# A new front with gates on 128 partitions, and VectorE in GpSimd's place for most subtractions

## The chip, the cores and the metric

One NeuronCore of a Trainium2 chip runs the whole program. The metric is the device time of one execution in microseconds, the median of several runs. TensorE (PE in the rows; PEld is its weight load) multiplies, VectorE (DVE) and ScalarE (ACT) do the elementwise work, GpSimd (POOL) helps out, and SyncE (SP) issues the DMAs.

## The reference

An mLSTM attention (batch 2, 8 heads, 768 positions, head size 40) feeds two MLP layers on 1536 tokens of width 320 with an inner width of 2048:

```python
for t in range(S):                                   # attention
    m_new = np.maximum(f_gate[:, :, t] + m, i_gate[:, :, t])
    f_stab = np.exp(f_gate[:, :, t] + m - m_new)
    i_stab = np.exp(i_gate[:, :, t] - m_new)
    C = f_stab * C + i_stab * outer(v_t, k_t);  n = f_stab * n + i_stab * k_t
    y[:, :, t] = sigmoid(o_t) * (C @ q_t) / max(|n @ q_t|, 1)
h = x @ w_in;  x = (h * clip(h + 3, 0, 6) / 6) @ w_out      # layer 1
h = x @ w_in;  out = (h * tanh(softplus(h))) @ w_out        # layer 2
```

(Broadcast indices are left out of the attention lines.)

## The kernel before, in words

**Attention** goes in six chunks of 128 positions (c = 0 to 5), each with two halves of 64. For a chunk, `loads` fetches q and k (`qke`, 1 MB) and then k, v and the o gate with tokens on partitions (`kvo`, 0.97 MB). The gates lie as 16 rows (batch and head) by 768 positions in `gio`. `scan_gates` (L657) runs a scan over them that gives the running maximum `mt`, in three parts (chunk 0, chunk 1, chunks 2 to 5), and follows it with three elementwise operations on the 16 rows; in the second part these three stand on GpSimd. `gates` (L672) transposes the result on TensorE (L679, L680) to 128 partitions by 32, makes the two factors with two sigmoids, a reciprocal and a product (`ist`), transposes the decay back (L701), and scans it over each half (L712 to L716: one scan over 128 columns, with the first column of each half moved to the tile `first`). `decays` spreads the decay into the 64 x 64 triangle of each row by 32 small matmuls and a scan (L840, L842; from chunk 2 on by a DMA through DRAM), `scores` is L815, `carry` builds the state (L942 and the `c` rows), `cross` is L890, `within` L985, and `mixture` (L989) ends with transposes (L1041) that give the layer input `x1` in a pair of fp32r tensors, high part and low part.

**Layers.** Every fp32 product is made of fp32r products of high and low parts. `prep` (L376) fetches a slot of weights (8 slots per layer; `ri` for w_in, 768 KB, `ro` for w_out, 640 KB) into one of four raw buffers, repairs it on ScalarE and VectorE (L365, L367), rounds the high part on ScalarE (L405, L417) and subtracts to get the low part (L411 to L428), on VectorE, GpSimd or TensorE by the lists `pool_rest` and `pe_rest`. The first 512 tokens (chunks 0 and 1) go through layer 1 a chunk at a time (`step1`: `ph` L465 up, `acc` L482 down, 8 slots for each chunk). The other two blocks go 512 wide (`step1_wide`: `phw`, `accw`). `act1` (L541) makes the activation, `r` and its parts `gh` and `gl`; the subtraction for `gl` (L554) stands on VectorE or GpSimd by the list `pool_low`. Layer 2 (`step2`: `qh`, `bcc`) follows for three blocks of 512 tokens.

**The order of the work** on each engine is written by the planner `Flow` while the program is built: every piece of work is a generator that asks for an engine with an estimated time and a priority (the lists in `P`; a lower number goes first), and the planner hands out engines and buffers in the order of its own clock. Engines then run that order strictly. DMAs all leave on the SP queue in planned order. While TensorE has nothing to do before the first `x1`, `keep_warm` (L1189) fills it with products of zeros (`pz`, L1198), as many as the planner's estimate of one fits into the gap.

Of the kernel before, what the change touches and what calls it, by code (L numbers as in the profile page):

```python
# [23 lines left out]
L = 128  # L24
# [17 lines left out]
P = {  # L42
    "const": [22, 11, 148],
    "gates": [81, 93, 41, 162, 127, 206],
    "load": [96, 281, 100, 227, 58, 130],
    "score": [9, 84, 243, 262, 211, 292],
    "value": [1, 29, 209, 138, 45, 241],
    "carry": [106, 73, 77, 59, 249, 250],
    "unit": [19, 171, 75, 86, 244, 228],
# [8 lines left out]
    ],  # L58
    "down2": [
        143, 60, 82, 259, 114, 54, 57, 63, 229, 156, 74, 6, 18, 44, 179, 139, 226, 173, 116, 155, 87, 183,  # L60
        203, 25, 72, 122, 53, 111, 115, 2, 151, 109, 27, 157, 3, 266, 263, 198, 24, 205, 32, 12, 88, 80,
        177, 89, 136, 90,
    ],
    "wide1": [
        140, 284, 67, 14, 33, 237, 185, 276, 235, 256, 288, 287, 215, 225, 248, 204, 191, 291, 184, 142, 17,
        79, 125, 144, 165, 34, 153, 39, 196, 293, 195, 102,
    ],
    "down1w": [
        35, 68, 290, 7, 105, 47, 30, 120, 251, 200, 297, 219, 50, 76, 124, 212, 152, 269, 16, 65, 99, 49,
        283, 26, 51, 15, 98, 94, 123, 37, 95, 277,  # L70
    ],
    "drain": [13, 217, 133, 126, 121, 56, 21, 48, 137, 71],
    "now": [4, 5],
    "window": [0.05],
    "on_value": [0, 0, 0, 0, 0, 2],
    "on_key": [0, 0, 0, 0, 0, 2],
    "on_gate": [0, 0, 0, 0, 0, 0],
    "pool_state": [0, 0, 0, 0, 0, 0, 0, 0, 0, 0, 1],
    "pool_rest": [
        0, 0, 0, 0, 1, 0, 0, 1, 0, 1, 1, 0, 0, 0, 1, 1, 0, 1, 0, 0, 0, 0, 1, 0, 0, 0, 0, 1, 0, 1, 1, 1,  # L80
    ],
    "pool_low": [
        0, 0, 0, 0, 0, 0, 0, 1, 0, 1, 1, 0, 1, 1, 1, 1, 1, 0, 0, 0, 0, 1, 1, 1, 1, 0, 1, 1, 1, 1, 1, 0, 1,
        0, 0, 0, 0, 0, 1, 0, 1, 1, 0, 0, 0, 1, 1, 0,
    ],
    "pe_rest": [0, 0, 0, 0, 0, 1, 0, 1, 0, 1, 0, 0, 0, 0, 0, 0],
    "pool_scan": [1, 0],
    "pe_low": [1, 1, 0, 0, 0, 0, 0, 0, 0, 0, 0, 0],
    "spread": [1, 1, 0, 0, 0, 0],
    "decay": [182, 253, 178, 141, 158, 104],  # L90
    "gload": [236, 40, 164, 175, 92, 181],
    "cross": [163, 83, 258, 103, 238, 66],
    "within": [214, 161, 36, 107, 112, 8],
# [50 lines left out]
class Flow:  # L144
# [4 lines left out]
    TO_PE, SWITCH = 0.13, 0.12  # L149
    TICK, COLUMNS = 10.24 / 3, 4000  # L150
    DMA = dict(rings0=2.0, slow=13e3, fast=20e3, until=3.0, start=1.9, end=0.5)

    def __init__(self):

        self.port = {DVE: 0.0, POOL: 0.0}
        self.engines = {PE: Engine(0.2), DVE: Engine(0.13), ACT: Engine(0.14), POOL: Engine(0.1), SP: Engine(0.0)}
        self.places = list(self.engines.values())
        self.now = 0.0
        self.rings, self.landed = [2.0] * 16, []
        self.tick, self.columns, self.fast = 0, 0.0, False  # L160
        self.fill, self.live, self.mode = None, 0, 0
# [76 lines left out]
    def transfer(self, place, t, size, n, issue):  # L238

        d = self.DMA  # L240
        rate = d["slow"] if t < d["until"] else d["fast"]
        for i in range(n):
            self.rings[i] = max(self.rings[i], t + d["start"]) + size / n / rate
# [30 lines left out]
    def grant(self, task, place, first):  # L274
        r = task.request
        task.last = None
        if isinstance(place, Slots):
            place.free.pop(0)
            task.t = first
        else:  # L280
            task.last = r[0]
            if r[0] == SP:
                self.now = self.transfer(place, first, r[1], r[3] if len(r) > 3 else 16, r[4] if len(r) > 4 else 0.45)
                self.set(r[2])
            elif r[0] == PE:
# [4 lines left out]
                start = first + (self.SWITCH if mode != self.mode else 0.0)  # L290
# [11 lines left out]
def mlstm_mlp_kernel(ctx, tc, qk, kvon, gates_io, w1i, w1o, w2i, w2o, eyes, consts, out):  # L302
# [145 lines left out]
    for j in range(len(BLOCKS) - 1):  # L448
        new_x()
# [198 lines left out]
    first = gpool.tile([16, L], F32, tag="first", name="first")  # L648
# [8 lines left out]
    def scan_gates(i, c0, c1):  # L657
        a, z = c0 * L, c1 * L
        n = (z - a) / 128
        r = slice(a, z)  # L660
        yield DVE, 0.12 + 0.27 * n, True
        V.tensor_tensor_scan(out=mt[:, a + 1 : z + 1], data0=fgt[:, r], data1=igt[:, r],
                             initial=mt[:, a : a + 1], op0=ALU.add, op1=ALU.max)
        on = i and P["pool_scan"][i - 1]
        eng = G if on else V
        for o, x, y, op in ((fgt, fgt, mt[:, a:z], ALU.add), (igt, igt, mt[:, a + 1 : z + 1], ALU.subtract),
                            (fgt, fgt, mt[:, a + 1 : z + 1], ALU.subtract)):
            yield flow.elementwise(on, 0.06 + 0.14 * n, 128 * n)
            tt(eng, o[:, r], x[:, r], y, op)
        flow.set(scanned[i])  # L670

    def gates(c):  # L672
# [5 lines left out]
        yield PE, 0.21, 128  # L678
# [4 lines left out]
        yield ACT, 0.16  # L683
        A.activation(s, p[:, 0:32], AF.Sigmoid, scale=-1.0)
        A.activation(g, p[:, 0:32], AF.Sigmoid)
        flow.put(in_a)
        yield DVE, 0.27
# [32 lines left out]
        ends = begins[:, :, HL - 1]  # L720
# [39 lines left out]
    def loads(c, before):  # L760
# [105 lines left out]
    def cross(c):  # L866
# [44 lines left out]
        flow.put(in_qke)  # L911
# [77 lines left out]
    def mixture(c):  # L989
# [45 lines left out]
        for b in range(B):  # L1035
# [138 lines left out]
    def start():  # L1174
        A.preload_act_table_set("sigmoid_and_others")
        flow.engines[ACT].free = 1.9
        V.memset(half, 0.5)
        V.memset(two, 2.0)
        V.memset(mt[:, 0:1], -1e30)
        flow.add(P["now"][0], keep_warm())  # L1180
        yield SP, 16e3, (ev := Event())
        SY.dma_start(out=gio[:, :, 0:L], in_=gates_io[:, :, 0:L])
        yield SP, 131e3, have["ident"]
        SY.dma_start(out=eye[:, 0:256], in_=eyes)
        flow.add(P["now"][0], scan_first(ev))
        flow.add(P["now"][0], spread_ident())
# [177 lines left out]
```

## Time and profile before

| | |
|---|---|
| median of 3 runs | 434.56 us (434.45 to 435.74) |
| the profiled execution | 434.39 us |
| its span, first to last instruction | 432.6 us |
| granted TensorE clock over the span | 1.000 |
| busy: PE, DVE, ACT, POOL | 98%, 70%, 62%, 14% |

Busy times of an engine are sums of what its instructions took; PE's 98% holds the fill as well. The profile's chain of waits gives 91% of the span to PE and 4% to DVE.

### The profile page before, as it was taken

How to read it: one execution, taken by the hardware profiler on the slowest of the kernel's cores; microseconds unless marked ns; L12 is line 12 of the kernel's file. 1: busy time of each engine (PE TensorE's matmuls, PEld its weight loads, DVE VectorE, ACT ScalarE, POOL GpSimd, SP SyncE). 2: the span in 40 equal slices, each digit the busy share in tenths (PEclk: the TensorE clock that was granted, in tenths of full speed). 3: DMA queues.
4: the chain of work that ended last, by engine and by line, in shares of the span. 5: the costliest groups of instructions: out<-in, count | busy, mean ns of one | idle time of the engine just before them, and what ended most of it. 6: DMA issues, size and time to landing. Idle time of an engine off the chain costs nothing.

```text
span 432.6 us, 9063 instructions
## 1 busy us (share of the span) xinstructions
PE 424.8 (98%) x3779; PEld 369.6 (85%) x3779; DVE 303.0 (70%) x532; ACT 268.9 (62%) x472; POOL 60.0 (14%) x54
## 2 busy tenths in 40 slices
PE   8999899999999999999999999999999999999996
PEld 6867899999998888887778888999999999899985
DVE  4989999999787322637976547766666666666664
ACT  5656676644443334069888358766686666767664
POOL 4010101181220134123036210000000000000000
PEclk9999999999999999999999999999999999999999
DMA  7958644651702027000782000000010000100001
GB/s 275 392 210 319 232 176 125 189 198 51 239 3 100 0 64 297 4 1 6 265 293 105 2 0 2 0 2 0 2 61 1 2 0 2 46 17 0 2 0 61
DMA packets 10040, 40.44 MB, mean 93 GB/s; under 512 B 2128, under 2 KB 3824, under 8 KB 9232
## 3 DMA queue, kind: packets, MB, share of 16 engines
q1 hardware_dynamic: 10000, 39.87, 25.8%
q8 instruction: 29, 0.48, 0.4%
q14 instruction: 11, 0.09, 0.1%
HBM read 37.64 MB, written 2.23 MB: 92 GB/s over the span
## 4 chain that ended last, share of the span: by engine, by line
PE 91%; DVE 4%; DMA 1%; ACT 1%; issue 1%; POOL 0%; DVEq 0%; ACTq 0%; POOLq 0%
PE qh L465 20%; PE accw L482 12%; PE phw L465 12%; PE acc L482 7%; PE ph L465 7%; PE bcc L1167 6%; PE bcc L1166 6%; PE bcc L1165 6%; PE pz L1198 4%; PE x L890 2%; PE s L815 1%; PE st L942 1%; DMA ri<-in_w2i 1%; PE z L985 1%; PE xp L1041 1%; PE fb L840 1%
## 5 line engine op out<-in xcount | busy, mean ns | idle before, releaser
L465 PE MATMUL qh<-x,wh 128*128 128x512 f32 x288 | 89.5, 392 | 0.0
L1116 DVE SCALAR_TENSOR_TENSOR u<-u,qh 128x512 f32<-128x512 f32 (+1 forms) x49 | 33.1, 676 | 39.1 <-ACT u L1114 39.1
L465 PEld LDWEIGHTS qh<-x,wh 128*128 128x128 f32 x288 | 52.3, 188 | 8.7
L1167 PE MATMUL bcc<-wd,gl 128*128 128x320 f32 x192 | 59.4, 309 | 0.2 <-DVE gl L1122 0.2
L1166 PE MATMUL bcc<-wd,gh 128*128 128x320 f32 x192 | 59.3, 309 | 0.0
L1165 PE MATMUL bcc<-wd,gh 128*128 128x320 f32 x192 | 59.3, 309 | 0.0
L465 PE MATMUL phw<-x,wh 128*128 128x512 f32 x192 | 58.9, 394 | 0.0
L1112 ACT ACTIVATE u<-u,two 128x512 f32<-128x512 f32 (+1 forms) x49 | 35.0, 715 | 30.8 <-DVE u L1110 30.7
L482 PE MATMUL accw<-ghw,wd 128*128 128x512 f32 x160 | 53.5, 399 | 0.0
L549 DVE SCALAR_TENSOR_TENSOR rw<-rw,phw 128x512 f32<-128x512 f32 x32 | 21.9, 686 | 38.4 <-ACT rw L547 38.2
L465 PEld LDWEIGHTS phw<-x,wh 128*128 128x128 f32 x192 | 35.7, 188 | 8.1
L547 ACT ACTIVATE rw<-phw,half 128x512 f32<-128x512 f32 x32 | 22.0, 689 | 26.5 <-PE phw L465 26.4
L482 PE MATMUL accw<-glw,wd 128*128 128x512 f32 x96 | 38.2, 398 | 0.2 <-DVE glw L309 0.2
L465 PE MATMUL qh<-x,wl 128*128 128x512 f32 x96 | 37.9, 395 | 0.0
L1165 PEld LDWEIGHTS bcc<-wd,gh 128*128 128x128 f32 x192 | 36.1, 188 | 2.1
L1166 PEld LDWEIGHTS bcc<-wd,gh 128*128 128x128 f32 x192 | 36.1, 188 | 1.9
L1106 ACT ACTIVATE u<-qh 128x512 f32<-128x512 f32 (+1 forms) x49 | 28.7, 587 | 14.3 <-PE qh L465 14.2
L1167 PEld LDWEIGHTS bcc<-wd,gl 128*128 128x128 f32 x192 | 36.1, 188 | 0.4 <-DVE gl L1122 0.4
L1122 DVE SCALAR_TENSOR_TENSOR gl<-u,gh 128x512 fp32r<-128x512 f32 (+1 forms) x49 | 33.1, 675 | 3.4 <-ACT gh L1120 3.3
L482 PEld LDWEIGHTS accw<-ghw,wd 128*128 128x128 f32 x160 | 29.5, 188 | 6.5
L1110 DVE SCALAR_TENSOR_TENSOR u<-u 128x512 f32<-128x512 f32 (+1 forms) x49 | 33.4, 681 | 1.6
L465 PE MATMUL ph<-x,wh 128*128 128x256 f32 x192 | 34.2, 288 | 0.0
(153 smaller groups left out, 838.7 us busy)
## 6 DMA issues: line engine op xcount, KB each, us to landing
ri<-in_w1i SPq DMA_DIRECT2D x8, 768.0 KB, 6.4
qke<-in_qk SPq DMA_DIRECT2D x6, 1024.0 KB, 5.0
ri<-in_w2i SPq DMA_DIRECT2D x8, 768.0 KB, 6.1
kvo<-in_kvon SPq DMA_DIRECT2D x6, 968.0 KB, 7.6
ro<-in_w1o SPq DMA_DIRECT2D x8, 640.0 KB, 5.2
ro<-in_w2o SPq DMA_DIRECT2D x8, 640.0 KB, 5.0
fb<-fzd SPq DMA_DIRECT2D x4, 512.0 KB, 4.3
out<-ot SPq DMA_DIRECT2D x12, 160.0 KB, 1.8
```

Of the source, the lines that this page charges most:

```text
L465: T.matmul(ph, a, b, start=(i == 0), stop=(i == len(seq) - 1))
L482: T.matmul(acc[k], a, b, start=start, stop=stop, skip_group_check=True)
L547: A.activation(r, ph, AF.Relu, bias=half, scale=1.0 / 6.0)
L549: V.scalar_tensor_tensor(out=r, in0=r, scalar=1.0, in1=ph, op0=ALU.min, op1=ALU.mult)
L1106: A.activation(u, ph, AF.Exp)
L1110: V.scalar_tensor_tensor(out=u, in0=u, scalar=2.0, in1=u, op0=ALU.add, op1=ALU.mult)
L1112: A.activation(u, u, AF.Ln, bias=two)
L1116: V.scalar_tensor_tensor(out=u, in0=u, scalar=0.5, in1=ph, op0=ALU.subtract, op1=ALU.mult)
L1122: V.scalar_tensor_tensor(out=gl, in0=u, scalar=-2.0, in1=gh.bitcast(F32), op0=ALU.mult, op1=ALU.subtract)
L1165: T.matmul(acc, a, hi, start=st, stop=False)
L1166: T.matmul(acc, a, lo, start=False, stop=False)
L1167: T.matmul(acc, b, hi, start=False, stop=sp)
```

## The change

- `first` and the three elementwise operations of `scan_gates` go, and with them the list `pool_scan`. `gates` now transposes f, i, and `mt` at both of its shifts (four transposes instead of two), copies the two `mt` parts to SBUF on ScalarE, and makes the sum and the differences on 128 partitions on VectorE. The prefix scan is two scans of 64 columns with a start value of 1, and the copy and the memset before it go.
- The first 128 positions of the gates are the first DMA of the kernel. Chunk 0's q, k, v come right behind the identity, ahead of the weights; before, one weight slot was first and four weight loads were ahead of chunk 0.
- q and k of chunk 1 get a place of their own, in the memory of the second `x` tile, so that their load no longer waits for chunk 0's `cross`; that `x` tile is made later.
- `pool_low` keeps 3 of its 23 ones (indices 7, 9, 10; that is until slot 2 of chunk 1). `pool_rest` loses five ones, all in layer 2 (indices 22, 27, 29, 30, 31) and keeps nine. The two operations on chunk 5's `kvo` that GpSimd had go to VectorE.
- All priorities are new, and some of the planner's estimates: DMA rate and latency, the time of a fill (`FILL`, at least 0.25 us), the switch between forms of matmul.

```diff
-    "load": [96, 281, 100, 227, 58, 130],
+    "load": [13, 280, 285, 47, 202, 246],
-    "prep0": [55, 62, 166, 0, 85, 160, 168, 52, 192, 149, 271, 213, 230, 234, 289, 285],
+    "prep0": [128, 86, 177, 129, 40, 114, 182, 120, 262, 62, 296, 278, 240, 289, 295, 266],
+    "first": [2],
-    "now": [4, 5],
+    "now": [6, 7],
-    "on_value": [0, 0, 0, 0, 0, 2],        # on_key alike
+    "on_value": [0, 0, 0, 0, 0, 0],
     "pool_rest": [
-        0, 0, 0, 0, 1, 0, 0, 1, 0, 1, 1, 0, 0, 0, 1, 1, 0, 1, 0, 0, 0, 0, 1, 0, 0, 0, 0, 1, 0, 1, 1, 1,
+        0, 0, 0, 0, 1, 0, 0, 1, 0, 1, 1, 0, 0, 0, 1, 1, 0, 1, 0, 0, 0, 0, 0, 0, 0, 0, 0, 0, 0, 0, 0, 0,
     "pool_low": [
-        0, 0, 0, 0, 0, 0, 0, 1, 0, 1, 1, 0, 1, 1, 1, 1, 1, 0, 0, 0, 0, 1, 1, 1, 1, 0, 1, 1, 1, 1, 1, 0, 1,
-        0, 0, 0, 0, 0, 1, 0, 1, 1, 0, 0, 0, 1, 1, 0,
+        0, 0, 0, 0, 0, 0, 0, 1, 0, 1, 1, 0, 0, 0, 0, 0, 0, 0, 0, 0, 0, 0, 0, 0, 0, 0, 0, 0, 0, 0, 0, 0, 0,
+        0, 0, 0, 0, 0, 0, 0, 0, 0, 0, 0, 0, 0, 0, 0,
-    "pool_scan": [1, 0],
...
-    DMA = dict(rings0=2.0, slow=13e3, fast=20e3, until=3.0, start=1.9, end=0.5)
+    FILL = 0.25
+    DMA = dict(first=1.5, rate=24e3, start=1.7, end=0.9)
...
-                    place.free = self.products(place.free, 0.214, 512)
+                    place.free = max(place.free + self.FILL, self.products(place.free, 0.214, 512))
...
     def scan_gates(i, c0, c1):
-        on = i and P["pool_scan"][i - 1]
-        eng = G if on else V
-        for o, x, y, op in ((fgt, fgt, mt[:, a:z], ALU.add), (igt, igt, mt[:, a + 1 : z + 1], ALU.subtract),
-                            (fgt, fgt, mt[:, a + 1 : z + 1], ALU.subtract)):
-            yield flow.elementwise(on, 0.06 + 0.14 * n, 128 * n)
-            tt(eng, o[:, r], x[:, r], y, op)
...
     def gates(c):
-        T.transpose(p[:, 0:16], fgt[:, q], ident[:16, :16])
-        T.transpose(p[:, 16:32], igt[:, q], ident[:16, :16])
+        for i, x in enumerate((fgt[:, q], igt[:, q], mt[:, q], mt[:, c * L + 1 : (c + 1) * L + 1])):
+            T.transpose(p[:, 16 * i : 16 * i + 16], x, ident[:16, :16])
-        A.activation(s, p[:, 0:32], AF.Sigmoid, scale=-1.0)
-        A.activation(g, p[:, 0:32], AF.Sigmoid)
+        A.copy(s, p[:, 32:64])
+        tt(V, p[:, 0:16], p[:, 0:16], s[:, 0:16], ALU.add)
+        tt(V, g.rearrange("t (x r) -> t x r", x=2), p[:, 0:32].rearrange("t (x r) -> t x r", x=2),
+           s[:, 16:32].unsqueeze(1).to_broadcast([128, 2, 16]), ALU.subtract)
+        A.activation(s, g, AF.Sigmoid, scale=-1.0)
+        A.activation(g, g, AF.Sigmoid)
...
-        V.tensor_copy(first.rearrange("r (a t) -> r a t", a=2)[:, :, 0:1], begins[:, :, 0:1])
-        V.memset(begins[:, :, 0:1], 0.0)
-        V.tensor_tensor_scan(out=pr, data0=pr, data1=first, initial=0.0, op0=ALU.mult, op1=ALU.add)
+        for a in range(2):
+            half_of = pr[:, a * HL : (a + 1) * HL]
+            V.tensor_tensor_scan(out=half_of, data0=half_of, data1=nothing, initial=1.0, op0=ALU.mult, op1=ALU.add)
...
     def loads(c, before):
-        yield in_qke
-        t["qke"] = apool.tile([128, B, 2, 4, L], F32, tag="qke", name=f"qke{c}")
-        yield SP, 852e3, ev["qk"], 13, 0.54
+        if c == 1:
+            flat = xpool.tile([128, 3072], F32, tag="x1", name="qke1")[:, 0 : 16 * L]
+            t["qke"] = flat.rearrange("p (b y h t) -> p b y h t", b=B, y=2, h=4)
+        else:
+            yield in_qke
+            t["qke"] = apool.tile([128, B, 2, 4, L], F32, tag="qke", name=f"qke{c}")
+        yield SP, 1049e3, ev["qk"], 16, 0.5
...
             if c // 2 == len(X):
-                yield ends[3]
+                yield ends[1 if c // 2 == 1 else 3]
                 new_x()
...
+        flow.add(P["first"][0], first_gates())       # the gates' first 128 positions, then their scan
```

## Rows read from the trace of the kernel before

**Rows 1.** Stretches: length, busy us (instructions) of PE, PEld, DVE, ACT, POOL; clock, DMA, GB/s.
```profile
40.00:126.00 86.00, 84.86 (x1293) 81.08 (x1290) 80.14 (x150) 48.78 (x99) 18.17 (x14) 1.00 0.47 158
126.00:200.00 74.00, 74.00 (x709) 60.11 (x708) 34.37 (x61) 31.27 (x56) 17.18 (x13) 1.00 0.18 68
200.00:250.00 50.00, 49.75 (x212) 39.31 (x212) 37.54 (x52) 39.01 (x56) 16.93 (x12) 1.00 0.42 145
250.00:432.60 182.60, 178.88 (x983) 160.64 (x981) 119.89 (x204) 125.38 (x213) 0.98 (x1) 1.00 0.03 12
...
5.40:126.00 120.60, 118.12 (x1871) 106.30 (x1869) 111.08 (x213) 71.44 (x149) 21.97 (x19) 1.00 0.58 208
5.40:118.00 112.60, 110.12 (x1813) 98.68 (x1811) 103.67 (x203) 67.81 (x141) 20.44 (x18) 1.00 0.61 221
...
10.00:15.00 5.00, 5.00 (x78) 3.92 (x76) 4.13 (x10) 3.83 (x10) 0.00 (x0) 1.00 1.02 427
```
**Rows 2.** Whom PE waited for, longest first: us in total, times, longest.
```profile
PE acc L482 <- DVE gl L309: 1.1, 1, 1.1
PE x L890 <- issue: 1.1, 1, 1.1
```
**Rows 3.** The chain that ended last, 0 to 45 us: start, us, what.
```profile
1.32 7.06 PE pz L1198 x20
...
40.07 3.06 PE ph L465 x24
```
**Rows 4.** PE groups by form: the fill.
```profile
L1198 PE MATMUL pz<-zeros 128*128 128x512 f32 x61 | 19.4, 453 | 1.3 <-POOL zeros L1195 1.3
```
**Rows 5.** Timeline to 24 us, chunk 0: start, us, engine, line, out<-in.
```profile
5.41 0.47 DVE L662 TENSOR_TENSOR_SCAN mt<-gio,mt 16x128 f32<-16x128 f32 x1 [4.50 <-DMA gio<-in_gates_io]
...
8.31 0.23 PE L679 MATMUL pg<-eye,gio 16*128 16x16 f32 x1
...
9.33 0.31 DVE L309 TENSOR_TENSOR ist<-ist,s 128x32 f32<-128x32 f32 x1
...
17.35 0.73 ACT L864 ACTIVATE kvo<-kvo 128x640 f32<-128x640 f32 x1
...
23.20 1.13 PE L942 MATMUL st<-kvo 64*64 64x41 f32 x64
```
**Rows 6.** SP's queue: start of issue, us, what.
```profile
0.74 0.39 SPq L357 DMA_DIRECT2D ro<-in_w1o  x1
...
6.02 0.57 SPq L775 DMA_DIRECT2D kvo<-in_kvon  x1
...
27.22 0.33 SPq L767 DMA_DIRECT2D qke<-in_qk  x1
```
**Rows 7.** DMA issues: KB each, median us to landing.
```profile
ri<-in_w1i SPq DMA_DIRECT2D x8, 768.0 KB, 6.4
gio<-in_gates_io SPq DMA_DIRECT2D x1, 16.0 KB, 4.1
```
**Rows 8.** DVE groups, 0 to 126 us: busy us, mean ns, idle before.
```profile
L842 DVE TENSOR_TENSOR_SCAN fb<-fb,eye 128x512 f32<-128x512 f32 x12 | 14.7, 1222 | 0.9 <-PE fb L840 0.7 <-DMA fb<-fzd 0.3
...
L309 DVE TENSOR_TENSOR gl<-r,gh 128x512 fp32r<-128x512 f32 x9 | 6.1, 679 | 0.0
...
L716 DVE TENSOR_TENSOR_SCAN pr<-pr,first 16x128 f32<-16x128 f32 x6 | 3.5, 576 | 0.0
...
L309 DVE TENSOR_TENSOR gio<-gio,mt 16x512 f32<-16x512 f32 x3 | 2.0, 672 | 0.0
...
L712 DVE COPY first<-pr 16x2 f32<-16x2 f32 x6 | 0.9, 150 | 0.2 <-ACT pr L708 0.2
...
L309 DVE TENSOR_TENSOR gio<-gio,mt 16x128 f32<-16x128 f32 x3 | 0.8, 274 | 0.0
```
**Rows 9.** POOL groups, 95 to 126 us, and one DVE row beside POOL.
```profile
L309 POOL TENSOR_TENSOR gl<-r,gh 128x512 fp32r<-128x512 f32 x4 | 5.2, 1288 | 18.7 <-ACT gh L552 18.7
...
49.30 1.59 DVE L309 TENSOR_TENSOR ist<-ist,s 128x32 f32<-128x32 f32 x1
```

More of the change, by code (lines that the diff above doesn't have):

```diff
@@ L42 @@
 P = {
-    "const": [22, 11, 148],
-    "gates": [81, 93, 41, 162, 127, 206],
-    "load": [96, 281, 100, 227, 58, 130],
[L46 to L49, printed above, removed]
[4 rows of a table removed]
+    "const": [56, 282, 228],
+    "gates": [21, 115, 54, 235, 105, 136],
+    "load": [13, 280, 285, 47, 202, 246],
+    "score": [17, 286, 109, 18, 269, 230],
+    "value": [9, 229, 288, 93, 293, 50],
+    "carry": [23, 142, 57, 100, 271, 80],
@@ L54 @@
+    "unit": [113, 52, 218, 27, 46, 268],
[4 rows of a table added]
     "up2": [
[3 rows of a table removed]
[3 rows of a table added]
     ],
     "down2": [
-        143, 60, 82, 259, 114, 54, 57, 63, 229, 156, 74, 6, 18, 44, 179, 139, 226, 173, 116, 155, 87, 183,
-        203, 25, 72, 122, 53, 111, 115, 2, 151, 109, 27, 157, 3, 266, 263, 198, 24, 205, 32, 12, 88, 80,
-        177, 89, 136, 90,
+        164, 88, 78, 87, 82, 197, 186, 99, 205, 29, 24, 181, 215, 188, 79, 14, 26, 179, 102, 42, 106, 157,
+        125, 196, 162, 22, 95, 169, 103, 151, 76, 199, 71, 68, 208, 89, 63, 203, 28, 131, 163, 41, 101, 37,
+        234, 187, 31, 108,
@@ L63 @@
     ],
     "wide1": [
-        140, 284, 67, 14, 33, 237, 185, 276, 235, 256, 288, 287, 215, 225, 248, 204, 191, 291, 184, 142, 17,
-        79, 125, 144, 165, 34, 153, 39, 196, 293, 195, 102,
+        34, 171, 150, 8, 11, 60, 81, 104, 121, 69, 233, 248, 133, 207, 245, 174, 156, 281, 267, 143, 147,
+        51, 183, 193, 94, 149, 70, 206, 172, 158, 250, 49,
     ],
     "down1w": [
-        35, 68, 290, 7, 105, 47, 30, 120, 251, 200, 297, 219, 50, 76, 124, 212, 152, 269, 16, 65, 99, 49,
-        283, 26, 51, 15, 98, 94, 123, 37, 95, 277,
-    ],
@@ L72 @@
-    "drain": [13, 217, 133, 126, 121, 56, 21, 48, 137, 71],
-    "now": [4, 5],
+        116, 189, 270, 33, 48, 32, 77, 74, 265, 255, 3, 239, 175, 144, 284, 145, 85, 1, 38, 45, 118, 84, 83,
+        55, 44, 184, 110, 73, 65, 231, 213, 208,
+    ],
+    "drain": [138, 0, 214, 200, 66, 260, 61, 119, 137, 148],
+    "first": [2],
+    "now": [6, 7],
     "window": [0.05],
-    "on_value": [0, 0, 0, 0, 0, 2],
-    "on_key": [0, 0, 0, 0, 0, 2],
+    "on_value": [0, 0, 0, 0, 0, 0],
+    "on_key": [0, 0, 0, 0, 0, 0],
@@ L85 @@
     ],
     "pe_rest": [0, 0, 0, 0, 0, 1, 0, 1, 0, 1, 0, 0, 0, 0, 0, 0],
-    "pool_scan": [1, 0],
     "pe_low": [1, 1, 0, 0, 0, 0, 0, 0, 0, 0, 0, 0],
     "spread": [1, 1, 0, 0, 0, 0],
[L90 to L93, printed above, removed]
+    "decay": [16, 192, 124, 201, 10, 176],
+    "gload": [279, 15, 212, 35, 236, 123],
+    "cross": [221, 58, 107, 134, 190, 53],
+    "within": [283, 287, 227, 294, 25, 261],
@@ L148 @@
     LANES = 8
-    TO_PE, SWITCH = 0.13, 0.12
+    TO_PE, SWITCH = 0.13, (0.12, 0.21)
     TICK, COLUMNS = 10.24 / 3, 4000
-    DMA = dict(rings0=2.0, slow=13e3, fast=20e3, until=3.0, start=1.9, end=0.5)
+    FILL = 0.25
+    DMA = dict(first=1.5, rate=24e3, start=1.7, end=0.9)
     def __init__(self):
@@ L158, in __init__ @@
         self.now = 0.0
-        self.rings, self.landed = [2.0] * 16, []
+        self.rings, self.landed = [self.DMA["first"]] * 16, []
         self.tick, self.columns, self.fast = 0, 0.0, False
@@ L240, in transfer @@
         d = self.DMA
-        rate = d["slow"] if t < d["until"] else d["fast"]
         for i in range(n):
-            self.rings[i] = max(self.rings[i], t + d["start"]) + size / n / rate
+            self.rings[i] = max(self.rings[i], t + d["start"]) + size / n / d["rate"]
         end = max(self.rings[:n]) + d["end"]
@@ L287, in grant @@
                     self.fill()
-                    place.free = self.products(place.free, 0.214, 512)
+                    place.free = max(place.free + self.FILL, self.products(place.free, 0.214, 512))
                 mode = r[3] if len(r) > 3 else 0
-                start = first + (self.SWITCH if mode != self.mode else 0.0)
+                start = first + (self.SWITCH[mode > 0] if mode != self.mode else 0.0)
                 self.mode = mode
@@ L446, in new_x @@
         X.append((xt[:, 0], xt[:, 1]))
-    for j in range(len(BLOCKS) - 1):
-        new_x()
+    new_x()
     x1 = [[Event() for _ in range(B)] for _ in range(NC)]
@@ L647, in mlstm_mlp_kernel @@
     fzd, istab, pend_sc, prefix = {}, {}, {}, {}
-    first = gpool.tile([16, L], F32, tag="first", name="first")
+    nothing = gpool.tile([16, HL], F32, tag="nothing", name="nothing")
     scanned = [Event() for _ in SCANS]
@@ L677, in gates @@
         p = bank(f"pg{c}")
-        yield PE, 0.21, 128
-        T.transpose(p[:, 0:16], fgt[:, q], ident[:16, :16])
-        T.transpose(p[:, 16:32], igt[:, q], ident[:16, :16])
+        yield PE, 0.4, 256
+        for i, x in enumerate((fgt[:, q], igt[:, q], mt[:, q], mt[:, c * L + 1 : (c + 1) * L + 1])):
+            T.transpose(p[:, 16 * i : 16 * i + 16], x, ident[:16, :16])
         g = istab[c] = gpool.tile([128, 32], F32, tag=f"ist{c}", name=f"ist{c}")
         s = gpool.tile([128, 32], F32, tag=f"s{c}", name=f"s{c}")
-        yield ACT, 0.16
-        A.activation(s, p[:, 0:32], AF.Sigmoid, scale=-1.0)
-        A.activation(g, p[:, 0:32], AF.Sigmoid)
+        yield ACT, 0.1
+        A.copy(s, p[:, 32:64])
+        yield DVE, 0.08
+        tt(V, p[:, 0:16], p[:, 0:16], s[:, 0:16], ALU.add)
+        yield DVE, 0.1
+        tt(V, g.rearrange("t (x r) -> t x r", x=2), p[:, 0:32].rearrange("t (x r) -> t x r", x=2),
+           s[:, 16:32].unsqueeze(1).to_broadcast([128, 2, 16]), ALU.subtract)
         flow.put(in_a)
+        yield ACT, 0.25
+        A.activation(s, g, AF.Sigmoid, scale=-1.0)
+        A.activation(g, g, AF.Sigmoid)
         yield DVE, 0.27
@@ L709, in gates @@
         yield have["clear"]
-        begins = pr.rearrange("r (a t) -> r a t", a=2)
-        yield DVE, 0.08, True
-        V.tensor_copy(first.rearrange("r (a t) -> r a t", a=2)[:, :, 0:1], begins[:, :, 0:1])
-        yield DVE, 0.03, True
-        V.memset(begins[:, :, 0:1], 0.0)
-        yield DVE, 0.33, True
-        V.tensor_tensor_scan(out=pr, data0=pr, data1=first, initial=0.0, op0=ALU.mult, op1=ALU.add)
+        for a in range(2):
+            half_of = pr[:, a * HL : (a + 1) * HL]
+            yield DVE, 0.2, True
+            V.tensor_tensor_scan(out=half_of, data0=half_of, data1=nothing, initial=1.0, op0=ALU.mult, op1=ALU.add)
         yield have["cst"]
@@ L719, in gates @@
         yield DVE, 0.1, True
-        ends = begins[:, :, HL - 1]
+        ends = pr.rearrange("r (a t) -> r a t", a=2)[:, :, HL - 1]
         tt(V, dd, cst[:, CM : CM + 8].unsqueeze(2).to_broadcast([16, 8, 2]), ends.unsqueeze(1).to_broadcast([16, 8, 2]), ALU.mult)
@@ L910, in cross @@
         yield done[c]["s"]
-        flow.put(in_qke)
+        if c != 1:
+            flow.put(in_qke)
     def carry(c):
@@ L1180, in start @@
         flow.add(P["now"][0], keep_warm())
-        yield SP, 16e3, (ev := Event())
-        SY.dma_start(out=gio[:, :, 0:L], in_=gates_io[:, :, 0:L])
         yield SP, 131e3, have["ident"]
         SY.dma_start(out=eye[:, 0:256], in_=eyes)
-        flow.add(P["now"][0], scan_first(ev))
         flow.add(P["now"][0], spread_ident())
@@ L1204, in keep_warm, with first_gates @@
         flow.put(in_acc)
-    def scan_first(ev):
+    def first_gates():
+        yield SP, 64e3, (ev := Event())
+        SY.dma_start(out=gio[:, :, 0:L], in_=gates_io[:, :, 0:L])
         yield ev
@@ L1228, in clear @@
         yield POOL, 0.2
-        G.memset(first, 0.0)
+        G.memset(nothing, 0.0)
         flow.set(have["clear"])
@@ L1236, in constants @@
     def constants():
-        yield SP, 7e3, have["cst"]
+        yield SP, 28e3, have["cst"]
         SY.dma_start(out=cst, in_=consts)
     def other_gates():
-        yield SP, 82e3, have["gates"]
+        yield SP, 328e3, have["gates"]
         SY.dma_start(out=gio[:, :, L:], in_=gates_io[:, :, L:])
```

2 lines of the change are left out of this document (1 added, 1 removed), and 12 rows, old and new, of the table P.

## Prediction

> **What bounds the kernel now.** I read the stretches first. From 40 us on TensorE is busy in nearly every microsecond: 84.86 of 86, then 74.00 of 74, 49.75 of 50, and 178.88 of 182.6 to the end, where the last products are drained and stored [rows 1]. The list of TensorE's waits has only two after the start that are worth a word, 1.1 us each [rows 2]. So behind 40 us time can be saved only by giving TensorE less to do, and the change takes no product away. Ahead of 40 us it is otherwise. The chain begins with fill (20 products of zeros in 7.06 us) and reaches the first layer product at 40.07 us [rows 3]; 61 fills take 19.4 us altogether [rows 4]. The front is where TensorE waits, and the reader is to see that its 98% hides that.
>
> Who makes it wait? From 5.4 to 126 us (about the end of the first block, 512 tokens) VectorE is busy 111.08 of 120.6 us, 92.1% [rows 1]. After that it has room: 34.37 of 74, 37.54 of 50, 119.89 of 182.6. So there are two bounds in series: the latency of chunk 0 until the first layer product, and VectorE's amount of work until the first block is done. A front that starts earlier is kept only as far as VectorE can also deliver earlier.
>
> **The change part by part.**
>
> *Loads.* Chunk 0's `kvo` was issued at 6.02 us behind four weight loads [rows 6], and its first reader, the sigmoid, ran at 17.35 us; the state products, which need it, ran at 23.20 us [rows 5]. Now 16 KB gates, 128 KB identity, 1024 KB q and k and 968 KB k, v, o go first, 2.14 MB. The rings moved 427 GB/s at their busiest [rows 1], which is 5.0 us; the 16 KB load took 4.1 us from issue to landing behind another load [rows 7], so with the first issue at 0.74 us [rows 6] I put chunk 0's landing at about 9 us, some 8 us earlier. The gates' first scan began at 5.41 us after a wait for its DMA [rows 5]; without a weight load ahead of it I take 1.5 us off (bounds: 0.45 us, the issue time saved, to 2.5 us).
>
> *Gate chain.* The first transpose ran at 8.31 us, right behind the 20 fills, and the product `ist` was done at 9.64 us [rows 5]. Three elementwise operations on 16 rows go from the chain (0.274 us each [rows 8]); a ScalarE copy, two small VectorE operations and two transposes come in. A 128x32 product took 0.31 us [rows 5]; three such are 0.9 us (bounds 0.5 to 1.5). With the transpose possible from about 4.8 us, `ist` is ready near 7.0 instead of 9.64 us.
>
> *First layer product.* From `ist` on the chain is 1.1 us of small products, two decay scans of 1.222 us [rows 8] one after the other, a scaling and the state products: 12.5 us at the earliest instead of 23.20. If the rest (16.9 us from the state products to 40.07) only moved along, the first layer product would stand at 29.4 us. The weights set a second floor. By the new priorities the first slot's w_in is only the sixth weight load; four raw buffers are there, so it waits until two are free, which I put at 17 us. Such a load took 6.4 us to land [rows 7], and with chunk 1's loads and one more ahead of it I put it near 25 us; its repair and split (about 4.8 us with hand-overs) end near 29.8 us. VectorE has weight work in between, as before, so I take 32 us: 8 us earlier, with ends 0 and 10.7 us.
>
> *VectorE's amount in the first block.* The list `pool_low` sends the subtractions of slots 4 to 7 of chunk 1 to VectorE: 4 by 0.679 us, 2.7 us more [rows 8]. The gates cost VectorE less: three operations of 0.274 and three of 0.672 us, six copies of 0.150 and six prefix scans (0.576 us on average) [rows 8], 7.2 us. In their place come 12 scans over half the length; a scan of 128 columns took 0.47 us [rows 5], so one of these lies between 0.24 and 0.47, and I take 0.33 us, 4.0 us in all. With 12 small operations near 0.18 us (between the copy's 0.150 and the product's 0.31) it is 6.2 us: 1.0 us less, with ends 3 less and 2 more. Beside GpSimd, VectorE's operations stretch: a 128x32 product that takes 0.31 us took 1.59 us at 49.30 us [rows 5, 9]. Most such places stay, because the weight subtractions of layer 1 and indices 7, 9 and 10 stay on GpSimd; of the removed ones I give back 0.5 us. The sum is 111.1 + 2.7 - 1.0 - 0.5 = 112.3 us. At the same 92.1%, starting at 3.9 us, it ends at 125.8 us, where it was 126: an early front would be paid back almost whole. But VectorE's last 7.4 us there (111.08 less 103.67 [rows 1]) are mostly chunk 4's, which the first block doesn't need, and which fit into the following stretch (34.37 of 74). With all of these later, it ends at 117.8 us. So the gain kept lies between 0.2 and 8.2 us, and I take the middle, 4.2 us: an order can defer chunk 4 but not all of it, since its loads and buffers follow in a ring.
>
> Here the Trainium skill has a rule that speaks against the change: Perfetto Trace Analysis, section Optimizing Scalar/DVE Operations, says that when VectorE is saturated, moving work to ScalarE or even GpSimd may make sense, and adds that GpSimd shares a read port with VectorE, so that this may not help. VectorE is near saturation here by rows 1. By the rule's first half the four moved subtractions are a loss of the 2.7 us worked out above; by its second half they are less than that, and the stretched product of rows 9 agrees with the second half.
>
> *TensorE.* Two more transposes per chunk, about 0.12 us for the pair after the first (the row of one shows 0.23 us with its drain [rows 5]); chunks 0 and 1 fall into the fill, four chunks cost 0.5 us (bounds 0 and 0.9). A different number of fills costs nothing as long as something else is late.
>
> *From 126 us on.* Some 16 subtractions of 0.679 us and two on chunk 5's `kvo` of about 0.8 us move to VectorE; it then has about 48 of 74 us in the first of these stretches. Between 200 and 250 us five more and the layer 2 weights make about 8 us, less what stretches there: some 43 of 50. TensorE hides both. Cost 0; if VectorE's burst at the start of layer 2's weights delays one activation, up to 1.1 us, the size of such a wait now [rows 2]. Taking GpSimd's 1.288 us [rows 9] out of the activation's path gains nothing where TensorE doesn't wait. Layer 2 and the end are the same instructions: 0.
>
> *Sum.* 434.39 (profiled execution) - 8.0 (first product earlier) + 3.8 (paid back to VectorE) + 0.5 (transposes) = 430.7. The median of the runs stands 0.17 us above the profiled execution, which holds the span of 432.6 us and 1.8 us around it: 430.9 us.
>
> **The rivals.**
>
> A, *kept whole*: the new order defers chunk 4 and TensorE is fed throughout from 32 us. For it: VectorE's room behind 126 us. Against it: 92% is already dense. 434.6 - 8.0 + 0.5 = 427.1 us.
>
> B, *paid back*: the first product comes earlier, but TensorE then waits for weights or VectorE between 45 and 110 us, and the first block ends where it did (125.8 us above). For it: VectorE's 80.14 of 86. Also the case in which the chain of chunk 0 isn't shorter because the first slot's weights come last. 434.6 - 0.2 + 0.5 = 434.9 us.
>
> C, *slower*: VectorE becomes the bound of the first block with more work than before. Place: from slot 4 of chunk 1 on, where the four subtractions join a stretch that is 93% busy. It decides as soon as VectorE's share in the first block falls under 92.0% with nothing deferred, (126 - 3.9) us for 112.3 us; at 90%, which a plan whose order waits more for its front would have, the block ends at 128.7 us, 2.7 us later, and the transposes add 0.5: 437.8 us. For it: two floors of 29 us leave little time for weights before the first product, and every early product needs some. Against it: the stretched operations show that GpSimd's help cost VectorE time as well.
>
> **How the numbers follow.** Forecast (428.6 to 433.2 us): 0.46. A: 0.21, with some of it lower than its number, down to 425. B: 0.17. C: 0.16. A measurement of this kernel can't tell less than 0.3% (1.3 us) from no change. Faster takes the forecast's range and A, and a little of B: 0.70. Same takes most of B and a little of C: 0.14. Slower is C with B's upper end: 0.16. The range leaves out A's lower end and C's upper half: 426.0 to 436.5 us.
>
> **What would show it.** Right: chunk 0's `kvo` read near 9 to 11 us; the first `ph` near 32 us and less than 15 us of fill; chunk 1's scores before 30 us instead of behind the load issued at 27.22 us [rows 6]; GpSimd idle from about 100 us; the first wide product 3 to 5 us earlier than before, and from there the same length to the end. Wrong: waits of TensorE on `gl`, `wl` or `wd` between 45 and 118 us that add up to what the front gained (B) or more (C); a first `ph` near 40 us; or a clock below the 1.00 of rows 1 while there are fewer fills.

## The result, and the profile after

After the change the kernel takes 440.97 us (440.29 to 441.53, 4 runs), beside 435.15 us (434.45 to 436.81) for the kernel before on the same chip: a ratio of 1.0139, 95% interval 1.0096 to 1.0183. It is slower; the forecast was 430.9 us. The profiled execution spans 439.1 us at a mean granted clock (the share of TensorE's full speed that it was given) of 0.979, where before it was 432.6 us at 1.000.

The page shows at once where to look. Each digit is a tenth, each column a fortieth of the span (11 us).

```profile
PE   8599899999999999999999999999999999999996
...
POOL 2100003260000000000000000000000000000000
PEclk9659999999999999999999999999999999999999
```

In the second and third column the granted clock is 0.6 and 0.5; before, every digit of that row is a 9. GpSimd's last subtraction ends at 110.7 us, where about 100 was foretold. The stretches of the front, kernel after (columns as in [rows 1]):

```profile
10.00:15.00 5.00, 1.63 (x8) 0.98 (x6) 2.94 (x3) 2.28 (x4) 2.09 (x2) 0.98 1.00 411
15.00:20.00 5.00, 3.53 (x43) 2.64 (x47) 4.53 (x10) 3.92 (x9) 0.00 (x0) 0.50 1.03 360
20.00:25.00 5.00, 5.00 (x81) 3.84 (x75) 3.10 (x9) 1.77 (x5) 0.00 (x0) 0.50 1.01 374
25.00:30.00 5.00, 5.00 (x69) 3.47 (x69) 2.33 (x8) 2.43 (x8) 0.00 (x0) 0.50 0.96 351
30.00:35.00 5.00, 5.00 (x125) 4.33 (x122) 4.55 (x12) 3.78 (x6) 0.00 (x0) 0.81 0.50 168
```

From 10 to 15 us TensorE was busy 1.63 us of 5 (before, 5.00 [rows 1]); from 15 to 30 us the clock is 0.50, that is 1.2 instead of 2.4 GHz. Between 20 and 30 us "busy" is 10.00 of 10 us, and yet much of it is loss, because each product takes longer. TensorE's timeline, kernel after, from 9.7 us on (start, us, engine, line, what, and in brackets the idle time before it and who ended that):

```profile
9.77 1.86 PE L1197 MATMUL pz<-zeros 128*128 128x512 f32 x7
16.47 1.43 PE L394 MATMUL pw<-ro,eye 128*128 128x320 f32 x2 [4.84 <-DVE ro L367]
...
19.29 1.93 PE L944 MATMUL st<-kvo 64*64 64x41 f32 x64
...
28.47 1.95 PE L987 MATMUL z<-kvo,fb 64*64 64x41 f32 x64
...
41.21 0.65 PE L464 MATMUL ph<-x,wh 128*128 128x256 f32 x2
```

Seven fills are queued, and then the product `pw` of a w_out weight that has not landed. TensorE waits 4.84 us at it. The 64 state products then take 1.93 us, where they took 1.13 [rows 5], and the first layer product comes at 41.21 us instead of 40.07 [rows 3]. Of fills there are 29 instead of 61 [rows 4]. The chain of waits tells whose weight it is (start, us, what):

```profile
4.32 9.96 DMA ro<-in_w1o
...
14.36 0.91 ACT top L365
15.27 0.12 ACT pr L708
...
15.62 0.80 DVE ro L367
...
16.47 1.43 PE pw L394 x2
```

A 640 KB load issued at 4.32 us landed 9.96 us later, among chunk 0's and other weights' loads. ScalarE's cast of it stands ahead of `pr`, chunk 0's own copy, so the chain of chunk 0 waits for the same load. The prediction had slot 0's late w_in as a floor, and in rival B the case that the first slot's weights come last; a w_out load at the head of ScalarE's and TensorE's queues, ahead of chunk 0's own work, was in none of its steps.

Nor do all of chunk 0's loads go ahead of the weights, as the list of the change and the prediction have it. SP's queue, kernel after:

```profile
2.12 0.43 SPq L768 DMA_DIRECT2D qke<-in_qk  x1
2.60 0.43 SPq L357 DMA_DIRECT2D ri<-in_w1i  x1
3.07 0.43 SPq L776 DMA_DIRECT2D kvo<-in_kvon  x1
...
4.32 1.42 SPq L357 DMA_DIRECT2D ro<-in_w1o  x3
```

A w_in load (768 KB) stands between `qke` and `kvo`.

Three milestones split the loss of 6.5 us in span. The first wide product `phw` comes at 126.68 us (before 122.24): 4.44 us. From there to the first layer 2 product `qh` it is 130.73 us (128.74): 1.99 us. The rest is 181.69 us (181.62): 0.07 us. (64 score products moved from ahead of `phw` to behind it, 1.2 us; by like work the first part lost that much more and the second that much less.)

### The profile page after: what moved, and what is told of

Read it like the earlier page. It is cut to its first block, busy times and chain, and to the rows that moved or that the text cites. A ratio compares the mean times of both kernels' runs of the same rounds, so it can differ in the third digit from the quotient of the medians.

```text
span 439.1 us, 8993 instructions
## 1 busy us (share of the span) xinstructions
PE 424.8 (97%) x3759; PEld 368.6 (84%) x3759; DVE 313.8 (71%) x561; ACT 269.5 (61%) x478; POOL 20.3 (5%) x22
## 2 busy tenths in 40 slices
DMA packets 10039, 40.43 MB, mean 92 GB/s; under 512 B 2128, under 2 KB 3824, under 8 KB 9232
## 4 chain that ended last, share of the span: by engine, by line
PE 76%; DVE 12%; ACT 4%; DMA 4%; issue 2%; SPq 1%; ACTq 0%; DVEq 0%
PE qh L464 20%; PE accw L481 11%; PE phw L464 11%; PE bcc L1169 6%; PE bcc L1168 6%; PE bcc L1167 6%; PE acc L481 5%; PE ph L464 3%; DMA ro<-in_w1o 2%; DMA ri<-in_w1i 2%; ACT top L365 1%; PE z L987 1%; PE pw L394 1%; PE st L944 1%; DVE ri L367 1%
## 5 line engine op out<-in xcount | busy, mean ns | idle before, releaser
L464 PE MATMUL ph<-x,wh 128*128 128x256 f32 x192 | 35.2, 290 | 0.6 <-DVE wh L309 0.6
```

The lines of the kernel that those rows point to most:

```text
L464: T.matmul(ph, a, b, start=(i == 0), stop=(i == len(seq) - 1))
```

## The experiments

Three theories. T: TensorE's idle time in the front brings the clock to 0.50, and the products behind it pay. V: VectorE pays for the subtractions. L: the new order is longer by itself. (Other letters in the expectations name rivals of one run, and are explained there.) All kernels here keep the order of instructions of the kernel they are made from, but for what the edit says.

**18 fills into the gap.** The kernel after:

```diff
...
             yield PE, n / 512 * 1.12, n * 5
+            if not flow.waited:                  # ahead of the first pw (comment added here)
+                flow.waited = True
+                for _ in range(18):
+                    flow.fill()
```

> The changed kernel with 18 more products of zeros on TensorE ahead of the first product that waits for a repaired weight; all orders else are as they were. The reading it tests (T): in the changed kernel TensorE stood idle 4.8 us before that product, its granted clock fell to 0.50 from about 15 to 32 us, and chunk 0's products, which took twice their time there, made the first layer product 5 us late. By T the clock stays at 1.00, chunk 0's last attention product (z) moves from 28.5 to 24 to 25 us, the first ph from 41.2 to 36 to 37 us, and the whole takes 434 to 436 us. Rival L (chunk 0 waits for loads and for ScalarE and VectorE in their order, the clock only follows): the clock stays up but the first ph stands within 1.5 us of 41.2, and the whole at 439.5 us or more. Rival V (the moved subtractions are the loss): no change, 441 us.

Measured 436.87 us, ratio to before 1.0078 [1.0034, 1.0121], span 434.3 us. The stretches of this kernel:

```profile
10.00:15.00 5.00, 5.00 (x72) 4.29 (x65) 3.07 (x4) 3.58 (x6) 2.03 (x2) 1.00 1.00 412
15.00:20.00 5.00, 5.00 (x88) 4.06 (x86) 4.88 (x12) 3.65 (x6) 0.06 (x1) 1.00 1.03 377
20.00:25.00 5.00, 5.00 (x105) 3.62 (x105) 4.10 (x14) 3.02 (x12) 0.00 (x0) 1.00 1.00 392
```

and its timeline:

```profile
11.55 5.95 PE L1202 MATMUL pz<-zeros 128*128 128x512 f32 x25
17.34 0.73 PE L399 MATMUL pw<-ro,eye 128*128 128x320 f32 x2
...
24.06 1.39 PE L992 MATMUL z<-kvo,fb 64*64 64x41 f32 x64
...
36.31 0.65 PE L469 MATMUL ph<-x,wh 128*128 128x256 f32 x2
```

`pw` comes no earlier (0.87 us later even, since in this execution the fills begin at 11.55 us instead of 9.77); but the clock is 1.00, `z` is 4.4 us earlier and `ph` 4.9 us. Products of zeros make the kernel 4.1 us faster (440.97 less 436.87; 3.7 us when each is taken beside its own runs of the kernel before). L and V, which expected 439.5 us or more, fall as the main cause. The kernel shows the same thing without an edit: two of its seven executions had a granted clock of 0.984 and 0.988 over the span and took 440.81 and 441.08 us, the other five, at 0.996 to 1.000, 436.26 to 437.92 us. (Where in the span it was lower is on record for none of the two. They widen the interval above, so that it overlaps that of the kernel after; that of the kernel with 14 fills below does not.) The median stays 0.9 us above the 436 that T expected at most; what is left is looked for below.

**The same 18 fills one place later**, behind the first `pw`, where the wait is over.

> The kernel after the change with the same 18 added fills as in the run that took 436.9 us, but one place later: behind the first product of the late weight instead of ahead of it, so TensorE still idles for 4.8 us and then has the fills. Theory T (the idle stretch brings the clock down): the granted clock falls to 0.50 from about 15 us as after the change, the fills take twice as long (some 8 us where the late weight's successors wait), the first layer product comes at 42 us or later, and the time is 441 us or more, up to 449. Rival N (the number of fills in the front decides, not their place): the clock is 1.00 by 20 us, 436 to 438 us.

442.23 us, ratio 1.0166 [1.015, 1.0181]; `ph` at 42.26 us. Its wait and its stretches:

```profile
17.07 1.43 PE L395 MATMUL pw<-ro,eye 128*128 128x320 f32 x2 [4.86 <-DVE ro L368]
...
18.59 5.57 PE L1202 MATMUL pz<-zeros 128*128 128x512 f32 x18
...
24.80 1.13 PE L949 MATMUL st<-kvo 64*64 64x41 f32 x64
```

```profile
15.00:20.00 5.00, 2.93 (x7) 2.05 (x8) 3.93 (x8) 3.93 (x9) 0.23 (x1) 0.50 1.03 380
20.00:25.00 5.00, 5.00 (x40) 3.89 (x40) 0.08 (x1) 0.76 (x1) 0.00 (x0) 0.87 0.65 259
25.00:30.00 5.00, 5.00 (x110) 3.59 (x101) 4.48 (x14) 2.10 (x8) 0.00 (x0) 1.00 0.41 134
```

The clock fell all the same, and the gain did not come: the number of fills is not it, and N falls. The fills took 5.57 us, not the 8 expected, for the clock rose again while they ran. Behind them chunk 0 runs at 1.00, but their own time now stands in its way: the state products come at 24.80 us instead of 19.29.

**14 and 9 fills ahead of `pw`.** The same edit with `range(14)` and `range(9)`.

> 14 added fills instead of 18 in the kernel after the change; the late weight's first product stood at 16.47 us without fills and at 17.34 us with 18, because the fills end later than the weight lands. Theory: 14 fills end near 16.6 us, the clock stays at 1.00, and the first layer product comes 0.5 to 0.9 us earlier than 36.31, if TensorE's queue sets it; 436.0 to 436.6 us. Rival (VectorE sets the front from 15 us on, where it is busy 20.2 of 21.3 us): the first layer product stays at 36.3 us or a little later, 436.7 to 437.2 us. If the clock falls below 1.00 with four fills fewer, 438 us or more.

> 9 added fills ahead of the late weight instead of 14 or 18, so that about 2.5 us of TensorE's 4.8 us of idle time are left. Theory T: the loss goes with how far the clock falls. If it stays at 1.00 the time is that with 14 fills, 435.5 to 436.5 us, and the first layer product stands near 36.5 us; if it falls for a part of the stretch, the first layer product stands between 37 and 41 us and the time between 437 and 440 us. Rival: if the added fills help in another way than by the clock (by shifting TensorE's order against the weights), half of them give half of the gain at a clock of 1.00, 438 to 439 us.

With 14: 435.8 us, ratio 1.0033 [1.0004, 1.0061], in the profiled execution at a clock of 1.00 throughout, the best of this order and still not faster than before. Here too three of twelve executions had a lower clock, 0.984 to 0.988, and took 438.26 to 439.12 us; the other nine, at 0.996 to 1.000, took 434.11 to 436.50. The interval overlaps that of 18 fills, so the two aren't told apart. The reason given for fewer fills, that they end sooner and `ph` comes earlier, fell: in the profiled execution the fills begin at 12.48 us, `ph` comes at 37.11, and in another kernel below, whose 18 fills begin at 9.77 us, they end 0.8 us before the weight is there. With 9: 440.43 us, ratio 1.0123 [1.01, 1.0145], no better than none by the intervals, and just above the 437 to 440 us expected for a clock that falls for a part:

```profile
16.21 0.83 PE L399 MATMUL pw<-ro,eye 128*128 128x320 f32 x2 [2.30 <-DVE ro L368]
...
28.23 1.95 PE L992 MATMUL z<-kvo,fb 64*64 64x41 f32 x64
...
40.81 0.65 PE L469 MATMUL ph<-x,wh 128*128 128x256 f32 x2
```

```profile
15.00:20.00 5.00, 3.54 (x51) 2.68 (x55) 4.77 (x11) 3.83 (x9) 0.00 (x0) 0.69 1.04 382
20.00:25.00 5.00, 5.00 (x73) 3.84 (x66) 3.07 (x10) 1.59 (x4) 0.00 (x0) 0.50 1.00 370
25.00:30.00 5.00, 5.00 (x74) 3.47 (x73) 2.12 (x7) 2.43 (x8) 0.00 (x0) 0.50 0.93 344
```

Half of the idle time gone gives none of the gain. The clock falls a little later and stays at 0.50 from 20 to 30 us under small products, although TensorE is busy all the time. That speaks against the rival (half the fills, half the gain at a clock of 1.00) and for the clock.

**The kernel before with 6 of its 61 fills**, the others not issued.

> The kernel before with the first 6 products of zeros kept and the other 55 left out; all orders else as they were. By T the granted clock falls to 0.50 somewhere before 20 us, the small products of chunk 0 take twice their time, the first ph moves from 40.0 to 42 to 45 us, and the whole takes 437 to 440 us. By L (waits for loads and VectorE set the front) the first ph stays within 1 us of 40.0 and the whole at 434.5 to 436 us; without fill in the way of products it could even gain up to 1 us.

436.71 us, ratio 1.0055 [1.0033, 1.0077]. Between the theories: the clock falls, to 0.54 from 10 to 15 us and to 0.50 from 25 to 35 us, but without fills in the way `z` comes earlier (26.68 instead of 29.40 us) and `ph` stays at 40.43. The expected `ph` of 42 us or more was a miss. I read this as slack: what the clock costs depends on whether the products that run slowly are waited for. No run here separates that from the missing fills.

**Who does the subtractions.** Each kernel with its own order, and the subtractions on the other's engine (one of the places; `pool_low` and chunk 5's `kvo` alike).

```diff
...
-        ei, eo = (G if P["pool_rest"][x] else V for x in (ji, jo))
+        ei, eo = (G if E["pool_rest"][x] else V for x in (ji, jo))   # E: the other kernel's lists
...
```

> The changed kernel with the moved subtractions (20 of the activations, 5 of weights, 2 on chunk 5) back on GpSimd, at the same place in the order. By V, which lays the loss on VectorE's added work, it takes 436 to 438 us. By T and L, for which the loss stands ahead of 41 us, it takes 440 to 442 us, a little more if activations now come late to TensorE (1.29 us instead of 0.68 each).

> The kernel before with the same subtractions on VectorE instead of GpSimd, at the same place in the order. By V it takes 437 us or more, with VectorE near 95% between 70 and 126 us. By T and L, and by the prediction's term (2.7 us more on VectorE in the first block, less 0.5, the rest hidden), it takes 434.5 to 437 us.

The order after with GpSimd's subtractions takes 447.22 us, ratio 1.0304 [1.0284, 1.0323], more than any theory expected. TensorE waits for the late weight as in the kernel after, and now for GpSimd besides:

```profile
PE pw L407 <- DVE ro L380: 4.9, 1, 4.9
PE accw L494 <- POOL glw L322: 4.6, 2, 2.6
```

The order before with VectorE's takes 434.09 us, ratio 0.9993 [0.9965, 1.002]. So in the old order the move costs nothing and gains nothing, and the new order needs it: V falls. What the change left on GpSimd are three `gl` and the low parts of five weights, four of layer 1 and one of layer 2 (`pool_rest` keeps seven ones, not the nine of the list of the change, and two of them go to TensorE by `pe_rest`). Moving these to VectorE as well, in the kernel with 18 fills:

> The kernel with the 18 added fills (436.9 us, profiled span 434.3) in the same order of all instructions, with the subtractions that the change left on GpSimd (indices of layer 1's weights, and gl 7, 9 and 10) on VectorE as well. Theory P: what is left of the loss, about 2 us, comes from VectorE operations stretched beside GpSimd (the scan that releases dd took 1.29 us beside a GpSimd subtraction of 1.94 us), so TensorE's wait on dd goes from 1.0 to under 0.3 us and the time falls to 434.5 to 436 us. Rival W: what is left is TensorE work that the old order had ahead of the first layer product and the new one has behind it (61 state products, 1.3 us) and the transposes (0.7 us): the waits may change by some tenths, the time stays within 436.3 and 437.5 us. Rival V2: VectorE is the bound of the first block, and the added subtractions (about 9 us more on it, less what stretches now) make it slower: 438 us or more.

439.89 us, ratio 1.01 [1.0069, 1.0132]; TensorE waits 2.0 us for `gl` and `gh` in the first block, where it waited 0.4, and 0.8 us for the late weight. The intervals of this kernel and the one with 18 fills overlap; the traces show the loss, with `phw` at 124.36 us instead of 121.55 from nearly the same `ph` (36.4 and 36.31). V2 (VectorE as the bound of the first block) it is, and P falls: the operations stretched beside GpSimd are no loss worth a cure.

**What sets the first layer product.** Two kernels with added fills: one leaves out five VectorE products ahead of `ph`, the other puts the work on the first three w_out weights behind chunk 0's state products.

> The kernel with 18 added fills, without five VectorE products of chunks 0 and 1 ahead of the first layer product: k by ul, the two decay products and the gate product of chunk 0, the value scaling of chunk 1 (3.8 us by the rows; these results are left out). Theory V3 (VectorE, busy 20.2 of 21.3 us from 15 us to the first layer product, sets the front): the first layer product comes 2.5 to 3.8 us earlier than 36.31, at 32.5 to 33.8 us, and because TensorE is 97% busy behind it the gain stays: 433 to 434.5 us. Rival B (a gain in the front is paid back to VectorE within the first block): the first layer product comes as early, but TensorE waits more behind it: 435.5 us or more. Rival L (weights or loads set it): the first layer product moves by less than 1 us, 436 to 437 us.

> The kernel with 16 added fills, and with the work on the first three w_out weights (casts, repairs, products) put behind chunk 0's state products on every engine, so that these no longer stand behind a load that lands at 14.3 us. Theory H (the head of the queues): the state products come at 15.5 to 16.5 us instead of 18.85 us. If the forecast's floor of 12.5 us plus 16.9 us for the rest was right, the first layer product follows them: 33.5 to 34 us, and the time is near 434.5 us. Rival V3 (VectorE's amount from 15 us on sets the front): the state products come as early, the first layer product within 0.7 us of 36.3 us, the time 436.3 to 437.5 us.

Without the five products: 436.73 us, ratio 1.0051 [1.002, 1.0082], `ph` at 36.01 us. With the chain first: 437.14 us, ratio 1.0063 [1.0033, 1.0094], state products at 15.95 us instead of 18.85, `ph` at 37.06. The first run rules out VectorE's amount (V3): 3.8 us less work, and `ph` moves by 0.3 us; time and `ph` are those of L. The second lands on the numbers that its rival expected, though V3's reason is gone, and H falls with its 434.5 us; its clock also fell for a while (0.92 and 0.73 in the stretches from 25 to 35 us), which makes its `ph` a little late. A chain that starts 2.9 us earlier brings nothing here. What stands in the way is seen in a chain of waits of the kernel without the five products (start, us, what):

```profile
20.33 6.77 DMA ri<-in_w1i
...
27.12 1.07 ACT top L366
...
28.21 0.64 DVE ri L368
...
29.09 0.82 DVE kvo L310
```

Slot 0's w_in is issued at 20.33 us, lands at 27.10, and is split by 33 us, in VectorE's order among other work. Its repair also stands ahead of `kvo`, chunk 0's last product, from which the transposes to `x` and then `ph` follow. This is the second floor of the prediction, some 3 us higher than it was put. But `ph` comes another 3 us behind it (36.01 us), and its last wait is for ScalarE's cast of `x`, the end of chunk 0's own chain. So the weight is argued as the cause, not shown: an earlier load was not tried.

**The rest of the loss.** The kernel with 14 fills reaches `phw` at 120.72 us, 1.5 us earlier than before, and `qh` at 251.86, 0.9 us later. Two groups of TensorE between these two, first the kernel before, then the one with 14 fills (busy us, mean ns, idle before):

```profile
L482 PE MATMUL accw<-glw,wd 128*128 128x512 f32 x90 | 35.8, 398 | 0.2 <-DVE glw L309 0.2
...
L815 PE MATMUL s<-qke 40*64 40x64 f32 x64 | 1.2, 222 | 0.0
```

```profile
L486 PE MATMUL accw<-glw,wd 128*128 128x512 f32 x90 | 35.9, 399 | 1.0 <-DVE glw L310 1.0
...
L821 PE MATMUL s<-qke 40*64 40x64 f32 x128 | 2.4, 222 | 0.0
```

The 64 score products (1.2 us) that now stand behind `phw` stood ahead of it, where TensorE was full as well: they change sides and cost nothing in all. So the whole stretch from `ph` to `qh` has to be compared. It takes 214.75 us (251.86 less 37.11), before 210.91 (250.98 less 40.07): 3.84 us more, which takes back the 2.96 us gained at `ph` and 0.9 us besides. TensorE is busy 211.99 us in it instead of 209.52, and idle 2.76 us instead of 1.39. Of the busy time, chunk 1's state products are 1.1 us: they stood ahead of `ph`, and now stand behind it. Before, then with 14 fills:

```profile
38.94 1.13 PE L942 MATMUL st<-kvo 64*64 64x41 f32 x64
```

```profile
37.11 0.66 PE L469 MATMUL ph<-x,wh 128*128 128x256 f32 x2
...
39.37 1.13 PE L949 MATMUL st<-kvo 64*64 64x41 f32 x64
```

The eight more transposes of the gates are 0.7 us. Of the idle time, 1.0 us is a wait for `dd` that was not there before, and the wait for `glw` grew from 0.2 to 1.0 us, while one for `gl` fell from 1.1 to 0.4. This is counted from the rows, not tried by a run.

## Why the prediction was wrong

**The step that failed** is the sentence "A different number of fills costs nothing as long as something else is late." It took fill as padding. Here fill is what holds the clock: with 4.84 us of idle time in place of it, the clock was 0.50 for some 15 us, and that cost 4.1 us (by the kernel with 18 fills) to 5.2 us (with 14), or 3.7 to 4.5 when each is taken beside its own runs of the kernel before. The prediction named "a clock below the 1.00" as a sign that would make it wrong, and gave it neither a price nor a chance. That step turned the kernel slower. That it is not faster with the clock at 1.00 either (435.8 us) has two more terms as its reason, the first layer product and what was kept of it.

**The first layer product at 32 us** would have failed without the clock as well: with the clock at 1.00 it comes at 36.31 us. The state products were put at 12.5 us at the earliest; they ran at 19.29 us, and at 18.85 with the clock at 1.00, because the late w_out stood ahead of them. The floor of the weights was put at 29.8 us with a landing at 25; in the kernel without the five products the landing is 27.1, and the split took 6 us between other work instead of 4.8. Chunk 1's scores, foretold before 30 us, stood at 32.29 us, and at 26.67 with the clock at 1.00.

**Right in the front:** the first scan began at 2.92 us, 2.5 earlier, the end of its bounds; `ist` was ready at 6.42 us (forecast 7.0); the 16 KB load landed in 2.1 us instead of 4.1 [rows 7]. `kvo` was first read at 11.48 us, half a us behind the forecast 9 to 11: the 2.14 MB of the sum left out the w_in load ahead of it, 1.8 us at the sum's 427 GB/s. In the kernel after all that bought nothing, since the next thing in TensorE's and ScalarE's queues was a weight that had not landed.

**Paid back:** the forecast gave back 3.8 of 8.0 us to VectorE. With the clock at 1.00 and 18 fills the 3.8 us gained at `ph` (40.07 to 36.31) were 0.7 at `phw` and a loss of 1.6 at `qh`. So B's outcome was nearer than the forecast, but not by B's means, as VectorE was not more loaded: it was busy 106.26 us up to `phw`, where it had been 107.78. By the count above, what ate the gain is products moved from the front, where TensorE had been filling, to stretches where it is full, and new waits of TensorE.

**C** named slower, and 437.8 us; that the time did rise is luck for it, since its place was wrong: the subtractions from slot 4 of chunk 1 on cost nothing in the old order (434.09 us).

**From 126 us on** was put at 0, up to 1.1 us if VectorE delays an activation; such a wait came (1.0 us for `glw` in all, before 0.2), and 64 score products from the stretch ahead, which no step held and which cost nothing in all. **The transposes** are there: behind `ph` the transposes of the gates are 16 instead of 8, 2.2 us of busy time in their groups instead of 1.5; the 0.5 us forecast was near. **Layer 2** and the end at 0: right, 0.07 us.

## What to carry to other kernels

Look at the granted clock of a front before counting its fill as idle time: each fill that a change takes out, and each wait at the head of TensorE's queue, may have to be priced at half speed for what follows until the clock is back. A chain that is made shorter gains only up to the next late thing in the same in-order queues, so work out the landing of the first weights with as much care as the chain itself. And ask what TensorE did in the time that is to be saved: products that stood there must now stand where it is full.

## What the runs showed of the hardware

- Filling 4.8 us of idle time with 14 fills kept the clock up in nine of twelve executions (0.996 to 1.000 over the span); leaving 2.3 us of it brought it to 0.50 in the profiled execution (0.983 to 0.988 over the span in all four), and there it stayed from 20 to 30 us, through small products, with TensorE busy throughout (5.00 of 5.00 us, twice). Under the 18 fills that came after the wait it was back within the stretch from 20 to 25 us (0.87).
- Long idle time is not the only way down, nor are fills the only way up. In the kernel with the chain first the clock was 0.92 and 0.73 in the stretches from 25 to 35 us, with no wait of TensorE above 0.73 us between 21 and 35 us. In the kernel before with 6 fills it rose from 0.54 (10 to 15 us) to 1.00 (15 to 20 us) without a fill. What decides is not shown.
- A row's clock is not all. In the profiled execution with 18 fills the first 32 decay products took 1.98 us at 6.71 us and the next 32 1.15 us at 10.44 us, both at a granted clock of 1.00; in the execution after the change both sets took 1.15 us, at 6.48 and 8.65 us. Why is open.
- Three w_out loads were issued between 4.32 and 5.74 us, with chunk 1's q and k behind them, and the first landed 9.96 us after its issue. The median to landing of `ro` was 8.8 us over the whole kernel, before 5.2.
